# Two blocks of w_in ahead of the first batch's x in the load queue, and another transfer model in the planner

## The chip, the cores and the metric

The program runs on one core of one Trainium2 chip. The metric is the device time of one execution in microseconds (us). The core has a matrix engine (PE, with its weight loads, PEld), a vector engine (DVE), an activation engine (ACT), a general engine (POOL), and a queue engine (SP) that here issues every transfer. Each engine takes its instructions strictly in the order in which they were written; an instruction that waits holds up all behind it on that engine.

## What is computed

Three stages in a row, in float32 inputs and outputs; the three weight matrices of the second and third stage come as float64.

```python
def _attn_ref(x, state):                       # x 8x8x512x64, state 8x8x32x64
    scores = scale * np.matmul(x, state.transpose(0, 1, 3, 2))
    a = softmax(scores); xread = np.matmul(a, state)
    scores2 = scale * np.matmul(state, x.transpose(0, 1, 3, 2))
    a2 = softmax(scores2); sread = np.matmul(a2, x)
    return np.concatenate([xread, sread], axis=2)

def _moe_ref(x, w_in, w_out, g_ln):            # 4352 tokens, 512 -> 1024 -> 512
    h = x @ w_in
    solu = h * softmax(h)
    ln = (solu - mean) / sqrt(var + 1e-06) * g_ln
    return ln @ w_out

def _moe2_ref(x, w_in, w_out):                 # 512 -> 2048 -> 512
    r = np.maximum(x @ w_in, 0.0)
    return (r * r) @ w_out
```

## The kernel before

**Phase 1** goes through eight batches of 512 tokens and then the 256 state tokens. Per batch: `scores` (PE products of `bdf`, the states, and `xT`, the transposed x; ACT copies them to `s_sb`), `max_t` (a DVE maximum, tile `m`), `emit_sT` (PE transposes; DVE maximum `mx` and subtraction into `a_sb`; ACT exponential in place; DVE sum, reciprocal; POOL scales), `emit_aT` (PE transposes back; ACT copies to `aT`), `emit_sw` (states times w_in, so that attention and the first dense layer become one product), `emit_l1` (PE products of `sw` and `aT` into `hps`; DVE maximum `hm`, ACT copy `u`), `solu_rest` (two ACT passes over 1024 columns with a DVE product between them, then POOL and DVE), `emit_lnT` (transposes, then ACT and DVE write the two halves of `lt`), and `emit_l2` (PE products of `lt` and `wo` into `y`). Beside that run `exp_t`, `emit_e`, `sread` and `emit_xs` for the state rows: ACT `eT`, PE `ep`, ACT copy back into `s_sb`, PE `srd`, ACT `sr`, PE `xsp`. Phase 1's results go to DRAM (`y_d`).

**Phase 2** runs over 9 groups of 512 (the last: 256) rows and 16 blocks `m` of 128 columns: `emit_l3` (PE products `h` of `wa[m]` and `yt`, line 907), `relu2` (ACT `r`, DVE `r*r`, ACT cast to the high part of `g`, DVE subtraction for its low part), and two steps later `emit_l4` (PE products `o` of `g` and `wb[m]`, line 922). Of each three products one needs the low part of `g`. The next group's rows come back from DRAM in two halves (`yraw`), which ACT casts and DVE or POOL subtracts (`yt`).

**The weights** are float64, so each block of 128x512 is loaded as 512 KB and decoded (`decode`): one ACT pass (line 293), two DVE passes (lines 296 and 299), for most weights an ACT cast into the high part and a subtraction into the low part, on POOL or DVE (line 249). The eight w_in blocks go to eight buffers of the pool `up`, so all eight can be in flight; they are the tiles `wi`, four for the first 512 columns (c = 0) and four for the rest. w_out's eight blocks (`wo`) follow; six can be in flight. Half of the third stage's weights are decoded in phase 1 and parked in DRAM; the other half (m = 8 to 15) are decoded in phase 2's first steps, with three `raw` buffers, which the halves of `yraw` share: a transfer is issued when the DVE pass that read its buffer has ended.

**What sets the order.** PE's order is written out by hand. The order on ACT, DVE, POOL and SP comes from a planner (`Flow`) while the program is built: it keeps a clock of its own, with a cost for each piece of work, and gives each engine the piece that is ready and due first; a second pass uses the due times that the first found. A transfer of `kb` KB is taken to occupy the resource "D" for kb/360 us, after earlier transfers, and to be ready 2.0 us later (`run`). The names of the steps below are the ones of the code. At the program's start SP issues the states and x of batch 0 (`load_x(0)`), then the eight w_in blocks, then `xn` (`load_xn(0)`), then w_out.

Of the kernel before, what the change touches and what calls it, by code (L numbers as in the profile page):

```python
# [23 lines left out]
class Flow:  # L24
# [16 lines left out]
    def __init__(self, plan=None):  # L41

        self.plan, self.made = plan, []
        self.now = 0.0
        self.end = 0.0
        self.warm = self.WARM_UP
        self.free = {"V": 0.0, "A": 0.0, "P": 0.0, "D": 0.0}
        self.tasks = []

    def run(self, eng, cost, ready, emit):  # L50
# [98 lines left out]
def attn_solu_relu2_kernel(  # L149
# [14 lines left out]
    nc = tc.nc  # L164
# [6 lines left out]
    B, P, T, _ = x_n.shape  # L171
    S = x_t.shape[3]
    HP = x_t.shape[2]
    H, D = 2 * HP, P // 2
# [13 lines left out]
    fl = Flow(plan)  # L188
# [33 lines left out]
    room = {"raw": 3, "dec": 3, "e": 2, "raw2": 3, "dec2": 2}  # L222

    def dma(out, in_, kb):
        return fl.run("D", kb / 360.0, 0.0, lambda e: nc.sync.dma_start(out=out, in_=in_))

    def take(name):
        def ok():
# [36 lines left out]
    def decode(dst_h, dst_l, src, pool=None, w=None, spare=False):  # L265

        raw, dec = ("raw2", "dec2") if spare else ("raw", "dec")
        if pool is None:
            yield take(raw)
            t = (ap_ if spare else raw_p).tile(
                [P, 512, 2], I32, tag=raw, name="raw", bufs=3
            )
        else:
            t = pool.tile([P, 512, 2], I32, tag="u", name="raw_u")
        tf = t.rearrange("p n c -> p (n c)")
        src = src.bitcast(I32)  # L280
        if len(src.shape) == 3:
            tf = tf.rearrange("p (k f) -> p k f", k=src.shape[1])
        f = dma(tf, src, 512)
        own = w is None
        if own:
            yield take(dec)
            w = (ap_ if spare else dec_p).tile(
                [P, 512], F32, tag=dec, name="dec", bufs=2 if spare else 3
            )
        w_i = w.bitcast(I32)  # L290
        hi, lo = t[:, :, 1], t[:, :, 0]
        h = hi.bitcast(F32)
        f = yield {"A": 0.66}, f, lambda e: nc.scalar.activation(
            out=w, in_=h, func=AF.Prelu, scale=2.0 ** -112, alpha=-(2.0 ** 32)
        )
        f = yield {"V": 0.46}, f, lambda e: nc.vector.tensor_scalar(  # L296
            out=w_i, in0=w_i, scalar1=3, scalar2=None, op0=ALU.logical_shift_left
        )
        f = yield {"V": 0.69}, f - fl.HOP, lambda e: nc.vector.scalar_tensor_tensor(  # L299
            out=w_i, in0=lo, scalar=29, in1=w_i, op0=ALU.logical_shift_right, op1=ALU.bitwise_or  # L300
        )
        if pool is None:
            give(raw)
        if not own:
            return f
        f = yield from split_w(dst_h, dst_l, w, f)
        give(dec)
        return f
# [14 lines left out]
    def load_x(b):  # L323
        bdf[b] = ap_.tile([P, G, 192], F32, tag="bdf", name="bdf", bufs=2)
        done["st", b] = dma(bdf[b], bd[b], 192)
        xT[b] = ap_.tile([P, HP, S], F32, tag="xT", name="xT")
        done["xT", b] = dma(xT[b], x_t[b], 1024)
# [439 lines left out]

    make_identity(nc, ident)
    nc.vector.memset(mhalf, -0.5)
    load_x(0)  # L770
    for c in range(C1):
        for k in range(KD):
            cs = slice(c * 512, (c + 1) * 512)
            done["wi", k, c] = fl.spawn(decode(
                None, None, w_in[k * P:(k + 1) * P, cs], pool=up, w=wi[k][:, cs],
            ), 5.0)
# [227 lines left out]
```

## Time and profile before

| what | value |
|---|---|
| time, median of 3 runs (range) | 1179.89 us (1179.64 to 1179.99) |
| profiled execution, its own time | 1181.55 us |
| its span, first to last instruction | 1179.5 us |
| PE busy | 1145.5 us (97%) |
| DVE, ACT, POOL busy | 534.7, 490.9, 177.8 us |
| PE's share of the chain that ended last | 90% |
| mean granted clock of PE | 0.991 |

PE is nearly always busy, so only its remaining gaps and its stretches at the lower granted clock can be won or widened. "Granted clock" (PEclk) is the share of full speed: 1.00 is 2.4 GHz, 0.50 is 1.2 GHz. PE's idle time lies in three places: the program's first 60 us, about one microsecond per batch in phase 1, and one gap at 470 us in phase 2.

### The profile page before, as it was taken

To read this page: it belongs to the slowest core of one execution; us is meant where nothing else is said; L and a number is where in the kernel's file an instruction comes from. 1 tells how busy PE (TensorE), PEld (TensorE's weight loads), DVE (VectorE), ACT (ScalarE), POOL (GpSimd) and SP (SyncE) were. 2 spreads that over 40 slices of the span, in tenths; PEclk is the share of its full clock that TensorE was granted. 3 is DMA by queue.
4 is the path that set the end of the run, shared out by engine and by line. 5 is a ranking of instruction groups with operands and counts; after the bars stand their busy time and mean duration, and the time that the engine had idled before them with its cause. 6 is when DMAs were issued, how large, how long until landed. Compare 5 with 4: busy or idle time off the path is not lost.

```text
span 1179.5 us, 14989 instructions
## 1 busy us (share of the span) xinstructions
PE 1145.5 (97%) x5992; PEld 910.7 (77%) x5992; DVE 534.7 (45%) x866; ACT 490.9 (42%) x875; POOL 177.8 (15%) x217
## 2 busy tenths in 40 slices
PE   4799999999999999999999999999999999999998
PEld 1377777777777687788888888888888888888887
DVE  6776876867764449423233232233232232232232
ACT  5866776767665456322222232232232232222222
POOL 1441433333243204100000000000000000010000
PEclk8999999999999999999999999999999999999999
DMA  9323253362331746011010020020020020010010
GB/s 358 126 79 111 94 186 108 114 214 77 111 121 63 298 144 214 18 33 40 1 51 21 1 72 1 1 72 1 1 72 1 1 72 1 1 54 1 1 37 18
DMA packets 32309, 88.00 MB, mean 75 GB/s; under 512 B 3824, under 2 KB 13040, under 8 KB 30192
## 3 DMA queue, kind: packets, MB, share of 16 engines
q1 hardware_dynamic: 32240, 87.05, 21.5%
q8 instruction: 47, 0.77, 0.3%
q14 instruction: 22, 0.18, 0.1%
HBM read 60.82 MB, written 26.21 MB: 74 GB/s over the span
## 4 chain that ended last, share of the span: by engine, by line
PE 90%; DVE 4%; ACT 3%; DMA 2%; issue 1%; SPq 0%; POOL 0%; ACTq 0%; DVEq 0%; POOLq 0%
PE o L922 31%; PE h L907 31%; PE y L675 14%; PE hps L614 8%; PE lnTp L640 2%; PE hps L360 1%; DMA raw<-w_in 1%; DMA raw_u<-w_in 1%; PE sTp L399 1%; DVE dec L299 1%; PE srd L471 1%; DVE hm L550 1%; ACT e L585 1%; DVE dec L296 1%; PE aTp L455 0%
## 5 line engine op out<-in xcount | busy, mean ns | idle before, releaser
L922 PE MATMUL o<-wb,g 128*128 128x512 f32 x1632 | 395.4, 391 | 2.9 <-ACT g L243 2.6
L907 PE MATMUL h<-yt,wa 128*128 128x512 f32 (+1 forms) x1728 | 394.2, 377 | 0.0
L907 PEld LDWEIGHTS h<-yt,wa 128*128 128x128 f32 x1728 | 313.3, 188 | 61.1
L922 PEld LDWEIGHTS o<-wb,g 128*128 128x128 f32 x1632 | 306.3, 189 | 66.8 <-ACT g L243 3.0
L891 DVE TENSOR_TENSOR r<-r 128x512 f32<-128x512 f32 (+1 forms) x144 | 109.0, 757 | 395.8 <-ACT r L884 395.7
L884 ACT ACTIVATE r<-h 128x512 f32<-128x512 f32 (+1 forms) x144 | 82.5, 573 | 405.5 <-PE h L907 405.3
L675 PE MATMUL y<-lt,wo 128*128 128x512 f32 (+1 forms) x864 | 218.8, 395 | 2.0 <-ACT lt L646 1.6
L675 PEld LDWEIGHTS y<-lt,wo 128*128 128x128 f32 x864 | 149.1, 190 | 38.5 <-issue 8.4
L249 DVE TENSOR_TENSOR g<-r,g 128x512 fp32r<-128x512 f32 (+1 forms) x144 | 95.6, 664 | 81.8 <-ACT g L243 76.0
L243 ACT CAST g<-r 128x512 fp32r<-128x512 f32 (+1 forms) x144 | 86.0, 597 | 101.8 <-DVE r L891 100.8
L249 POOL TENSOR_TENSOR yt<-yraw,yt 128x1024 fp32r<-128x1024 f32 (+1 forms) x8 | 18.2, 2277 | 558.2 <-ACT yt L243 558.2
L614 PE MATMUL hps<-sw,aT 128*128 128x512 f32 x368 | 97.9, 415 | 0.0
L614 PEld LDWEIGHTS hps<-sw,aT 128*128 128x128 f32 x368 | 69.0, 189 | 23.6 <-issue 6.8
L649 DVE SCALAR_TENSOR_TENSOR lt<-lnTp,g_sb,lt 128x512 fp32r<-128x512 f32 (+1 forms) x72 | 51.1, 710 | 38.4 <-ACT lt L646 38.0
L550 DVE TENSOR_REDUCE hm<-hps 128x1 f32<-128x512 f32 x68 | 45.8, 688 | 44.1 <-PE hps L614 34.8
L243 ACT COPY u<-hps 128x512 f32<-128x512 f32 x68 | 39.6, 582 | 55.1 <-DVE hm L550 54.9
L646 ACT ACTIVATE lt<-lnTp,g_sb 128x512 fp32r<-128x512 f32 (+1 forms) x72 | 47.9, 667 | 12.6 <-PE lnTp L640 12.6
L579 DVE SCALAR_TENSOR_TENSOR u<-u,e 128x1024 f32<-128x1024 f32 x34 | 42.5, 1251 | 9.9 <-ACT e L574 9.9
L585 ACT ACTIVATE e<-u,nmu 128x1024 f32<-128x1024 f32 x34 | 39.2, 1152 | 15.8 <-DVE nmu L582 14.9
L640 PE MATMUL lnTp<-ident,u 128*128 128x128 f32 x272 | 41.8, 274 | 1.6 <-DVE a_sb L249 1.2
L640 PEld LDWEIGHTS lnTp<-ident,u 128*128 128x128 f32 x272 | 32.7, 140 | 11.1 <-issue 2.4
L574 ACT ACTIVATE e<-u,nmx 128x1024 f32<-128x1024 f32 x34 | 39.1, 1150 | 3.0 <-DVE nmx L567 2.9
(83 smaller groups left out, 714.7 us busy)
## 6 DMA issues: line engine op xcount, KB each, us to landing
raw<-w_out SPq DMA_DIRECT2D x24, 512.0 KB, 5.2
out<-osb SPq DMA_DIRECT2D x34, 256.0 KB, 2.2
xT<-x_t SPq DMA_DIRECT2D x8, 1024.0 KB, 4.9
xn<-x_n SPq DMA_DIRECT2D x8, 1024.0 KB, 6.6
y_d<-ys SPq DMA_DIRECT2D x16, 512.0 KB, 2.9
raw<-w_in SPq DMA_DIRECT2D x16, 512.0 KB, 4.3
w_d<-w2s SPq DMA_DIRECT2D x16, 512.0 KB, 3.0
yraw<-y_d SPq DMA_DIRECT2D x16, 512.0 KB, 5.5
```

The costliest lines, as they stand in the source:

```text
L243: nc.scalar.copy(out=out, in_=in_)
L249: return lambda e: eng_of[e].tensor_tensor(out=out, in0=in0, in1=in1, op=ALU.subtract)
L550: one({"V": 0.68}, lambda e, c=c, ps=ps: nc.vector.tensor_reduce(out=m2[:, c:c + 1], in_=ps, axis=AX.X, op=ALU.max)),
L585: f = yield {"A": 1.16}, f, lambda e: nc.scalar.activation(out=e_, in_=u, func=AF.Square, bias=nmu, accum_out=vs)
L614: nc.tensor.matmul(out=ps, lhsT=lhsT(i, k), rhs=rhs(j, k)[:, cs], start=(k == 0 and n == 0), stop=(k == n_k - 1 and n == len(passes) - 1),)
L640: nc.tensor.transpose(ps[:, t, :], u_t[key, t][:, k * P:(k + 1) * P], ident)
L649: f = yield {"V": 0.1 + nt * 0.155}, f, lambda e: nc.vector.scalar_tensor_tensor(out=o[:, 1], in0=pf, scalar=gk, in1=o[:, 0].bitcast(F32), ...
L675: nc.tensor.matmul(out=ps, lhsT=wo[k][:, w, c * P:(c + 1) * P], rhs=o[:, a], start=(k == 0 and i == 0), stop=(k == K1 - 1 and i == 2),)
L884: first = one({"A": 0.06 + n / 1000}, lambda e: nc.scalar.activation(out=r, in_=hps, func=AF.Relu))
L891: f = yield {"V": 0.15 + n / 960}, first["done"], lambda e: nc.vector.tensor_tensor(out=r, in0=r, in1=r, op=ALU.mult)
L907: nc.tensor.matmul(out=hps, lhsT=wa[m][:, w, k, :], rhs=yt[j][:, a, k, :], start=(k == 0 and i == 0), stop=(k == KD - 1 and i == 2),)
L922: nc.tensor.matmul(out=ops[j][t], lhsT=g[:, a, t * P:(t + 1) * P], rhs=wb[m][:, w, :], start=(m == 0 and i == 0), stop=(m == K2 - 1 and i ...
```

## The change

Batch 0's states and x are issued after the first two w_in blocks. The planner's transfers become faster (400 instead of 360 KB per us), and the first cannot start before 2.2 us. Since all orders but PE's come from the planner, both numbers reorder work all over the program. PE's order is the same as before, row for row.

```diff
-        self.free = {"V": 0.0, "A": 0.0, "P": 0.0, "D": 0.0}
+
+        self.free = {"V": 0.0, "A": 0.0, "P": 0.0, "D": 2.2}
...
-        return fl.run("D", kb / 360.0, 0.0, lambda e: nc.sync.dma_start(out=out, in_=in_))
+        return fl.run("D", kb / 400.0, 0.0, lambda e: nc.sync.dma_start(out=out, in_=in_))
...
-    load_x(0)
     for c in range(C1):
         for k in range(KD):
+            if (c, k) == (0, 2):
+                load_x(0)
```

Behind the new lines each line number is one or two higher than before.

**Place 1: the start.** DVE before, from the first w_in block on (`wi_122` to `wi_125` are the four w_in tiles, `m` the maximum of the scores, the last row the subtraction of the first half):

```order
L296 TENSOR_SCALAR wi_122<-wi_122 128x512
L299 SCALAR_TENSOR_TENSOR wi_122<-raw_u,wi_122 128x512
L371 TENSOR_REDUCE m_202<-s_sb 128x1
L296 TENSOR_SCALAR wi_123<-wi_123 128x512
L299 SCALAR_TENSOR_TENSOR wi_123<-raw_u,wi_123 128x512
L296 TENSOR_SCALAR wi_124<-wi_124 128x512
L299 SCALAR_TENSOR_TENSOR wi_124<-raw_u,wi_124 128x512
L371 TENSOR_REDUCE m_214<-s_sb 128x1
```

and now:

```order
L297 TENSOR_SCALAR wi_122<-wi_122 128x512
L300 SCALAR_TENSOR_TENSOR wi_122<-raw_u,wi_122 128x512
L297 TENSOR_SCALAR wi_123<-wi_123 128x512
L300 SCALAR_TENSOR_TENSOR wi_123<-raw_u,wi_123 128x512
L297 TENSOR_SCALAR wi_124<-wi_124 128x512
L300 SCALAR_TENSOR_TENSOR wi_124<-raw_u,wi_124 128x512
L372 TENSOR_REDUCE m_209<-s_sb 128x1
L297 TENSOR_SCALAR wi_125<-wi_125 128x512
```

The first maximum moved from behind the first block to behind the third. ACT a little later, before (`dec<-raw` is the first pass over a w_out block, `a_sb` the exponential of the second half):

```order
L243 COPY sw<-hps 128x512
L293 ACTIVATE wi_125<-raw_u 128x512
L243 COPY sw<-hps 128x512
L418 ACTIVATE a_sb<-a_sb 128x512
L243 COPY aT<-aTp 128x512
L293 ACTIVATE dec<-raw 128x512 x3
```

and now:

```order
L294 ACTIVATE wi_125<-raw_u 128x512
L244 COPY sw<-hps 128x512
L294 ACTIVATE dec<-raw 128x512
L419 ACTIVATE a_sb<-a_sb 128x512
L244 COPY aT<-aTp 128x512
L294 ACTIVATE dec<-raw 128x512 x3
```

The first pass over w_out's first block moved ahead of the exponential.

**Place 2: the end of batch 0's first layer.** ACT before, from the last but one pass over 1024 columns ahead of the copy of `ep` (wo_129 to wo_131 are w_out's fourth to sixth block):

```order
L574 ACTIVATE e,es<-u,nmx 128x1024
L243 COPY u<-hps 128x512
L574 ACTIVATE e,es<-u,nmx 128x1024
L243 COPY s_sb<-ep 128x512
L243 COPY u<-hps 128x512
L585 ACTIVATE e,vs<-u,nmu 128x1024
L574 ACTIVATE e,es<-u,nmx 128x1024
L489 ACTIVATE sr<-srd,l_186 128x64 x2
L349 ACTIVATE s_sb<-sps 128x512
```

and now:

```order
L586 ACTIVATE e,vs<-u,nmu 128x1024
L244 COPY u<-hps 128x512
L586 ACTIVATE e,vs<-u,nmu 128x1024
L244 COPY u<-hps 128x512
L244 COPY s_sb<-ep 128x512
L575 ACTIVATE e,es<-u,nmx 128x1024 x2
L244 CAST wo_131<-dec 128x512
L350 ACTIVATE s_sb<-sps 128x512
L490 ACTIVATE sr<-srd,l_186 128x64 x2
```

The last two exponentials moved behind the copy of `ep`, and the casts of w_out's fifth and sixth block came into this stretch from a later one, where one of them stood just ahead of the first `lt`.

**Place 3: phase 2, where the last w2 blocks and the next group's `yraw` come in.** ACT before (`r_4730` and `g_4731` are those of block m = 6 of the first group):

```order
L243 CAST wa15_4434<-dec_4687 128x512
L243 CAST yt_4481<-yraw_4704 128x1024
L884 ACTIVATE r_4730<-h2_4701 128x512
L243 CAST wb13_4431<-dec_4707 128x512
L293 ACTIVATE dec_4726<-raw_4720 128x512
L243 CAST g_4731<-r_4730 128x512
L243 CAST yt_4481<-yraw_4735 128x1024
```

and now (`r_4737` and `g_4738` are the same block):

```order
L244 CAST wa15_4434<-dec_4679 128x512
L244 CAST yt_4486<-yraw_4691 128x1024
L244 CAST wb13_4431<-dec_4695 128x512
L886 ACTIVATE r_4737<-h2_4709 128x512
L294 ACTIVATE dec_4715<-raw_4712 128x512
L244 CAST yt_4486<-yraw_4728 128x1024
L244 CAST g_4738<-r_4737 128x512
```

The cast of the second half of `yraw` moved ahead of the cast of `g`, and on DVE its subtraction moved ahead of the low part of `g` in the same way. In the steps before, the first pass of a w2 block stands one block earlier against `r` and `g`, and one subtraction (wa11's) went from DVE to POOL. In phase 1's batches 2 to 5, likewise, a w2 block's first pass and cast stand ahead of a `u` copy and an `lt`.

## Rows read from the trace of the kernel before

**Rows 1.** Windows: stretch, its length, busy us (count) per engine, PEclk, DMA.
```profile
20.00:30.00 10.00, 5.90 (x25) 2.11 (x24) 9.61 (x16) 6.85 (x13) 3.62 (x3) 0.50 1.05 388
...
47.00:59.00 12.00, 7.42 (x65) 3.77 (x57) 9.62 (x20) 11.20 (x26) 7.09 (x13) 0.86 0.53 192
...
61.00:64.00 3.00, 3.00 (x10) 2.41 (x10) 2.97 (x5) 1.10 (x3) 2.13 (x2) 0.50 0.02 5
...
434.00:470.00 36.00, 36.00 (x160) 29.52 (x158) 33.61 (x42) 24.00 (x41) 15.35 (x11) 1.00 0.69 218
...
474.00:477.00 3.00, 3.00 (x8) 2.33 (x8) 3.00 (x3) 1.60 (x4) 1.80 (x1) 0.50 0.01 4
...
480.00:1150.00 670.00, 670.00 (x3002) 556.62 (x3001) 197.83 (x277) 173.15 (x284) 18.17 (x8) 1.00 0.08 23
```

**Rows 2.** Waits of PE from 70 us to the end: total us, times, longest.
```profile
PE sTp L399 <- ACT s_sb L243: 4.4, 6, 0.7
```

**Rows 3.** Timeline of ACT at the start: start, us, what, [idle before <- releaser].
```profile
9.88 0.66 ACT L293 ACTIVATE wi<-raw_u 128x512 f32<-128x512 f32 x1 [0.85 <-DMA raw_u<-w_in]
...
11.34 0.68 ACT L293 ACTIVATE wi<-raw_u 128x512 f32<-128x512 f32 x1 [0.32 <-DMA raw_u<-w_in]
...
20.66 0.63 ACT L418 ACTIVATE a_sb<-a_sb 128x512 f32<-128x512 f32 x1 [1.73 <-DVE a_sb L249]
...
21.67 0.67 ACT L293 ACTIVATE dec<-raw 128x512 f32<-128x512 f32 x1
22.81 0.68 ACT L293 ACTIVATE dec<-raw 128x512 f32<-128x512 f32 x1 [0.47 <-DMA raw<-w_out]
```

**Rows 4.** Timeline of DVE at the start.
```profile
8.51 0.43 DVE L296 TENSOR_SCALAR wi<-wi 128x512 int32<-128x512 int32 x1 [7.67 <-ACT wi L293]
...
18.13 1.90 DVE L296 TENSOR_SCALAR wi<-wi 128x512 int32<-128x512 int32 x3
```

**Rows 5.** Timeline of PE at the start.
```profile
24.42 1.11 PE L455 MATMUL aTp<-ident,a_sb 128*128 128x128 f32 x4 [4.10 <-POOL a_sb L428]
```

**Rows 6.** Timeline of PE and ACT from 42.9 to 60 us.
```profile
42.95 0.60 PE L442 MATMUL ep<-ident,eT 128*128 128x128 f32 x4
...
43.73 1.16 ACT L574 ACTIVATE e<-u,nmx 128x1024 f32<-128x1024 f32 x1
...
44.87 0.58 ACT L243 COPY s_sb<-ep 128x512 f32<-128x512 f32 x1
...
45.50 0.65 PE L471 MATMUL srd<-xn,s_sb 128*32 128x64 f32 x32 [1.37 <-ACT s_sb L243]
...
58.23 0.63 ACT L243 CAST wo<-dec 128x512 fp32r<-128x512 f32 x1
...
59.50 0.73 PE L675 MATMUL y<-lt,wo 128*128 128x512 f32 x2 [1.57 <-ACT lt L646]
```

**Rows 7.** Timeline of all engines from 464 to 474 us.
```profile
464.21 0.34 SPq L225 DMA_DIRECT2D yraw<-y_d  x1
...
467.92 0.33 SPq L225 DMA_DIRECT2D yraw<-y_d  x1
468.00 1.05 ACT L243 CAST yt<-yraw 128x1024 fp32r<-128x1024 f32 x1 [0.55 <-DMA yraw<-y_d]
...
472.02 0.62 ACT L243 CAST g<-r 128x512 fp32r<-128x512 f32 x1 [0.97 <-DVE r L891]
...
472.69 0.73 PE L922 MATMUL o<-wb,g 128*128 128x512 f32 x2 [2.58 <-ACT g L243]
472.88 1.05 ACT L243 CAST yt<-yraw 128x1024 fp32r<-128x1024 f32 x1 [0.24 <-DMA yraw<-y_d]
472.96 0.68 DVE L249 TENSOR_TENSOR g<-r,g 128x512 fp32r<-128x512 f32 x1
473.70 4.16 PE L922 MATMUL o<-wb,g 128*128 128x512 f32 x10 [0.28 <-DVE g L249]
...
473.96 1.23 DVE L249 TENSOR_TENSOR yt<-yraw,yt 128x1024 fp32r<-128x1024 f32 x1 [0.31 <-ACT yt L243]
```

## The prediction

> **What bounds the kernel now.** I read the windows first [rows 1]: from 434 to 470 us and from 480 to 1150 us PE is busy without a gap, so nothing that the change moves there counts unless it is late enough to open one. Over the whole of 70 us to the end, the list of PE's waits has, beside the gap at 470, little more than one entry: 0.7 us in six batches, for a copy that waits for PE itself [rows 2]. So a change of order on the other engines can move the time in three places: the start, the stretch to 60 us where ACT is the full engine (11.20 of 12 us in the window from 47 us [rows 1]), and the gap of 2.58 us at 470 us in phase 2 [rows 7]. In the first and the third the granted clock matters as well. It was 0.50 from 20 to 30 us, from 61 to 64 us and from 474 to 477 us [rows 1], each time behind a stretch in which PE had waited, and it was 1.00 in the full stretches. In a 0.50 stretch PE does half the work, so being late there costs half, and a wait that falls into one costs half of itself.
>
> The sum below is made against the profiled execution, 1181.55 us with a span of 1179.5. The median of the runs is 1179.89, so a difference found there is carried over to the median as it is. A measurement of this kernel can tell about 0.2%, 2.4 us, from no change.
>
> **Part A, the start.** The third w_in block has the same bytes ahead of it as before (states, x, two blocks), so it still arrives at about 11.3 us [rows 3], and so do all transfers behind it. What changes hands are the places in front: the first two blocks now come before 9.9 us, and x comes where the second block came, at about 9.9 us [rows 3]. The gain: the DVE passes over two blocks fall into time in which DVE sat idle for 7.67 us [rows 4]. The price: x's scores come later, and their first maximum, a pass of about 0.7 us, now stands behind the third block, in the stretch in which DVE had no room. Part of that is covered, since three passes of 0.42 us took 1.90 us there, 0.6 us of it waiting [rows 4]. So the subtraction of the second half comes 0 to 0.7 us later. It is not what decides. ACT's exponential of that half, which started at 20.66, now stands behind the first pass over w_out's first block. That pass ran at 21.67, and its block had only just come: the second came at 22.81, after a wait; at 1.46 us from block to block (11.34 less 9.88) the first came at 21.35 or later, and at 21.67 at the latest, so about 21.5 [rows 3]. The exponential then starts at 21.5 + 0.6 = 22.1 instead of 21.1 at the least: about 1.0 to 1.4 us later than 20.66, of which I take 1.0, because the passes queued on DVE cover the rest. The chain behind it (DVE sum, POOL, PE's transpose at 24.42 [rows 5]) moves with it: 25.4. PE runs at 0.50 until 30 us [rows 1], so 1.0 us late is 0.5 us of work at full clock. **A: +0.5**, between 0 (transfers that start quicker) and +1.0 (no halving).
>
> **Part B, 30 to 62 us.** The copy of `ep` stood behind an exponential that ran from 43.73 to 44.87, though PE had ended `ep` at 43.55; PE waited 1.37 us for that copy and went on at 45.50 [rows 6]. Now two exponentials stand behind the copy instead, so with A's 0.5 the copy can start at 44.05 to 44.5: 0.4 to 0.8 earlier, of which A's delay has been taken. Against this, the casts of w_out's fifth and sixth block, 0.63 each [rows 6], come into a stretch in which ACT is full, ahead of the copies of the scores for which PE waits next. The fifth's left a place at 58.23, right before the first `lt`, for which PE waited until 59.50 [rows 6], but a first pass of 0.67 takes that place. So PE's first `y` product comes between 0.6 earlier (the copy's gain) and 1.3 later (both casts). Around 61 to 64 us the clock is 0.50 [rows 1], so half of it counts. And A's half microsecond is partly lost in this part anyway, since ACT, not PE, sets its pace. **B: -0.2**, between -0.8 and +0.7.
>
> **Part C, phase 2 at 470 us.** Before, ACT cast `g` of block 6 at 472.02, PE went on at 472.69 with the products that need only the high part, waited again, and went on at 473.70 when the low part (472.96 + 0.68) was there [rows 7]. ACT's cast of the second half of `yraw` came after it, at 472.88, as soon as that transfer had landed. Now this cast stands ahead. The transfer is issued when a DVE pass has freed its buffer, at 467.92, and cannot be cast before 472.88 if DVE gets there no sooner. DVE is busy 33.61 of the 36 us before [rows 1], with the same passes in another order: one subtraction (0.7) fewer, and one more on POOL, during which DVE's passes get longer. I take no change of pace, 0.7 either way. Then: cast of `yraw` 472.88 to 473.93, cast of `g` to 474.55, subtraction of `yraw` on DVE (1.23) from 473.96 to 475.15, low part of `g` to 475.75. PE goes on with the low part at 475.75 instead of 473.70: 2.05 later. Any wait that the later `g` of block 5 opens falls inside this one, since PE only gets to the same gate later. The clock gives some back: from 474 to 477 it was 0.50 with PE busy throughout [rows 1], and now PE stands still for about half of that, if the low stretch stays where it was. A second low stretch behind the longer wait would take that and more. I give back 0.7. **C: +1.3**, between +0.3 (landing and DVE earlier, all of the clock's gift) and +2.8 (2.05 and a low stretch moved onto full work).
>
> A transfer of 512 KB took 3.8 us from issue to its cast at the one place and 5.0 at the other [rows 7], more than the planner's 3.28. The Trainium skill speaks for the planner here: DMA: Bandwidth & Descriptors, section Anatomy of one DMA, has about 2.0 us of fixed cost plus the bytes at 436 GB/s, which would be an estimated 3.2 us. By that figure the second half would have landed at 471.1 us and the new place of its cast would cost next to nothing; the trace does not agree, and the measured 5.0 decides.
>
> **Part D, the rest.** In four batches a w2 block's first pass and cast (0.67 + 0.62) stand ahead of an `lt`. PE waited for no `lt` after 70 us: the only entry of weight is another copy [rows 2], so the cover is the work that PE has queued; without it each would cost up to 0.7. I take 0, between -0.3 and +1. In phase 2's later groups the casts of `yraw` move ahead of `r`; PE has no gap there [rows 1], and `g` is due two steps later, so 0.
>
> **The sum.** +0.5 - 0.2 + 1.3 + 0 = +1.6 us: 1183.15 us for an execution like the profiled one (span 1181.1), and 1179.89 + 1.6 = **1181.5 us** for the median, which is 0.14% and inside what counts as the same. With the parts' bounds half used on either side, this case reaches from 1179.9 to 1183.5.
>
> **The rivals.**
>
> *The wait at 470 us grows in full (slower).* One mechanism: the `yraw` cast holds up `g`, and the clock falls after the wait rather than during it. C is then 2.8, A and B together +0.8: 1179.89 + 3.6 = 1183.5. For it: DVE was nearly full before 470 us, and blocks are decoded one step earlier against `r` and `g`, so that `g` of block 5 comes late too. Against it: in the trace the low stretch began at 474, in the wait's wake, and a longer wait overlaps it. It decides from the point where PE's restart passes about 476 us.
>
> *The start wins (faster).* Mechanism: DVE's early passes and a quicker start of the transfers pull the second half's exponential ahead rather than behind, and the copy of `ep` 0.8 earlier carries through to the first `y`, so that the wait before 59.50 (1.57) goes and with it the low stretch from 61 to 64 us, which holds 3 us at half speed and so costs 1.5. That is -0.8 - 0.8 - 1.5 = -3.1, plus at the least 0.3 for C: 1177.1. For it: 7.67 us of idle DVE at the start is the largest gap that the change can fill. Against it: the first pass over w_out stands ahead of the exponential and is bound to a transfer that does not come earlier.
>
> *Nothing that counts.* Transfers land as the planner has them, 3.8 us as the first half did: the second half lands at 467.92 + 3.8 = 471.7, its cast ends at 472.8, PE's low part comes at 474.6, 0.9 later than before, half of it at 0.50, and A and B cancel: 1180.3. This is also the skill's figure made into a mechanism, with its time from the rows.
>
> **How the numbers follow.** Forecast 0.36, slower rival 0.34, faster rival 0.18, nothing that counts 0.12. The edges are 1177.5 and 1182.25 us. Of the forecast's 0.36 I count 0.07 as beyond the upper edge and 0.02 beyond the lower, and of the slower rival's 0.34 I count 0.05 inside: slower 0.36, faster 0.17 (a little of it falls short of the edge), same 0.47. The range for 8 in 10 reaches into both rivals: from 1177.4 to 1185.0, the upper end being the slower rival with A and D at their bounds (+1.5).
>
> **What would show it.** Right in A: the second `aTp` of the start at about 25.4, behind an exponential that follows a pass over w_out. Right in B: PE's second `srd` between 44.6 and 45.2, first `y` within 1 us of 59.5. Right in C: in phase 2, ACT's `yraw` cast directly ahead of `g`, PE waiting for `g` about 2 us longer at 470 to 476, and the low part behind a subtraction of `yraw`. Wrong in C, and the forecast with it: PE's wait there no longer than 2.9 us in all, or two low stretches of the clock instead of one. Wrong in A and B: PE's first `y` before 58.5 or after 61, or the low stretch at 61 us gone.

## The result

| kernel | median us (runs) | ratio to before, 95% interval | PE's first `h` of phase 2, us | from there to the end of the span, us |
|---|---|---|---|---|
| before | 1179.94 (4) | 1 | 429.12 | 750.4 |
| after | 1193.55 (4) | 1.0107 (1.0095 to 1.0119) | 435.66 | 756.5 |

The changed kernel is 13.6 us slower by the medians. Its profiled execution took 1193.97 us, with a span of 1192.2 us, which is 12.7 us more than the span of before; the places of the loss below are read from these two profiles. The forecast was 1181.5 us, with a range up to 1185.0: the time lies far outside it.

PE runs the same products in the same order in both, so the start of one and the same product is a ruler. One profile stands for each kernel: seven profiles with the same start as after put the first `y` at 60.07 to 60.74 us, so differences of less than about 0.7 us say little. PE's first product of phase 2, in before and then in after:

```profile
429.12 8.34 PE L907 MATMUL h<-yt,wa 128*128 128x512 f32 x36
```

```profile
435.66 8.34 PE L909 MATMUL h<-yt,wa 128*128 128x512 f32 x36
```

Phase 1 thus lost 6.5 us and phase 2 another 6.2. At the first `y` (59.50 before [rows 6], 60.12 after) only 0.6 was lost, so the batches carry 5.9. After's windows (columns as in [rows 1]) over the batches and at the beginning of phase 2:

```profile
64.00:440.00 376.00, 365.73 (x2402) 276.56 (x2401) 233.45 (x429) 236.28 (x442) 114.46 (x163) 1.00 0.37 129
440.00:500.00 60.00, 52.97 (x217) 41.62 (x216) 45.80 (x55) 32.01 (x54) 21.13 (x15) 0.94 0.47 151
```

PE's waits in after from 70 us to the end (total, times, longest), where before had the entry of [rows 2], 0.9 us for `sw`, and the gap of [rows 7]:

```profile
PE sTp L400 <- ACT s_sb L244: 4.8, 6, 1.2
PE o L924 <- DVE g L250: 3.8, 3, 1.4
PE o L924 <- ACT g L244: 3.2, 2, 3.0
PE hps L615 <- ACT s_sb L350: 2.8, 3, 1.3
...
PE hps L615 <- ACT u L244: 0.6, 1, 0.6
```

The chain that ended last, PE's at 90% in before, now reads:

```profile
PE 80%; DVE 7%; DMA 7%; ACT 5%; issue 2%; SPq 0%; ACTq 0%; DVEq 0%
```

New are the waits of `hps` for `s_sb` and `u`; those for the low part of `g` grew from 0.3 to 3.8 us. All of these are written by ACT or DVE behind something else. What that is, ACT's own waits from 70 to 440 us show: before, then after.

```profile
ACT dec L293 <- DMA raw<-w_in: 12.0, 6, 3.7
ACT dec L293 <- DMA raw<-w_out: 7.4, 3, 3.1
```

```profile
ACT dec L294 <- DMA raw<-w_in: 14.4, 5, 3.8
ACT dec L294 <- DMA raw<-w_out: 12.7, 5, 3.8
```

ACT stands idle for weight blocks that have not landed, 19.4 us before (1.3 of it, at 440 us, for a block of phase 2, the rest for parked blocks) and 27.1 us after, and behind some of these passes PE's work queues up. The largest single case, after, all engines from 154 to 172 us:

```profile
155.08 0.33 SPq L226 DMA_DIRECT2D xn<-x_n  x1
...
155.50 0.41 SPq L226 DMA_DIRECT2D w_d<-w2s  x1
...
156.01 0.38 SPq L226 DMA_DIRECT2D raw<-w_out  x1
...
165.08 0.66 ACT L294 ACTIVATE dec<-raw 128x512 f32<-128x512 f32 x1 [3.83 <-DMA raw<-w_out]
165.64 0.57 ACT L244 COPY u<-hps 128x512 f32<-128x512 f32 x1
...
166.26 1.66 PE L615 MATMUL hps<-sw,aT 128*128 128x512 f32 x6 [0.55 <-ACT u L244]
...
166.95 0.62 ACT L244 CAST w2s<-dec 128x512 fp32r<-128x512 f32 x1 [0.15 <-DVE dec L300]
167.48 1.15 ACT L575 ACTIVATE e<-u,nmx 128x1024 f32<-128x1024 f32 x1
...
168.62 0.57 ACT L350 ACTIVATE s_sb<-hps 128x512 f32<-128x512 f32 x1
...
169.25 1.68 PE L615 MATMUL hps<-sw,aT 128*128 128x512 f32 x6 [1.33 <-ACT s_sb L350]
```

The block is issued behind a 1 MB load and a 512 KB store and lands 9.0 us later. ACT comes to its pass at 161.25, waits 3.83, and only then copies the second `u`, which PE waits for; the cast and the exponential behind it make `s_sb` late, and PE waits again. Ahead of this place PE was 0.86 us later than in before (its `y` products start at 164.05 against 163.19), behind it 3.32 us (its next transposes start at 170.76 against 167.44), so 2.5 of the batches' 5.9 us are lost here. In before ACT has done `u`, `lt` and the exponential by the time it comes to the same pass, the transfer has landed, 7.9 us after its issue, and PE's products are in one piece:

```profile
161.16 0.59 ACT L243 COPY u<-hps 128x512 f32<-128x512 f32 x1 [0.78 <-DVE hm L550]
161.65 0.69 ACT L646 ACTIVATE lt<-lnTp,g_sb 128x512 fp32r<-128x512 f32 x1
...
162.23 1.15 ACT L574 ACTIVATE e<-u,nmx 128x1024 f32<-128x1024 f32 x1
...
163.36 0.66 ACT L293 ACTIVATE dec<-raw 128x512 f32<-128x512 f32 x1
...
164.69 2.91 PE L614 MATMUL hps<-sw,aT 128*128 128x512 f32 x12
```

In phase 2, after, all engines around the `yraw` cast that the prediction spoke of:

```profile
467.72 2.57 PE L924 MATMUL o<-wb,g 128*128 128x512 f32 x10 [1.25 <-DVE g L250]
...
475.29 2.57 PE L924 MATMUL o<-wb,g 128*128 128x512 f32 x10 [1.37 <-DVE g L250]
...
477.34 0.33 SPq L226 DMA_DIRECT2D yraw<-y_d  x1
...
478.46 1.65 DVE L893 TENSOR_TENSOR r<-r 128x512 f32<-128x512 f32 x1
...
482.00 1.04 ACT L244 CAST yt<-yraw 128x1024 fp32r<-128x1024 f32 x1 [3.02 <-DMA yraw<-y_d]
482.95 0.61 ACT L244 CAST g<-r 128x512 fp32r<-128x512 f32 x1
483.08 1.23 DVE L250 TENSOR_TENSOR yt<-yraw,yt 128x1024 fp32r<-128x1024 f32 x1 [1.91 <-ACT yt L244]
...
483.62 1.22 PE L924 MATMUL o<-wb,g 128*128 128x512 f32 x2 [3.04 <-ACT g L244]
...
484.16 1.27 POOL L250 TENSOR_TENSOR wb<-dec,wb 128x512 fp32r<-128x512 f32 x1 [4.61 <-ACT wb L244]
484.22 1.76 DVE L250 TENSOR_TENSOR g<-r,g 128x512 fp32r<-128x512 f32 x1
...
486.04 4.53 PE L924 MATMUL o<-wb,g 128*128 128x512 f32 x10 [1.20 <-DVE g L250]
```

`r` was squared by 480.11, so `g` could have been cast then; it stood behind a transfer that landed at 482.00. A window over 484 to 491 us shows what followed, PE at about half of its clock (0.55) for 7 us, where before had 3 us of it [rows 1]:

```profile
484.00:491.00 7.00, 5.80 (x15) 4.08 (x15) 5.60 (x8) 3.49 (x7) 2.55 (x2) 0.55 0.00 0
```

### The profile page after: what moved, and what is told of

The parts are those of the page before. It is cut to its first block, busy times and chain, and to the rows that moved or that the text cites. A ratio compares the mean times of both kernels' runs of the same rounds, so it can differ in the third digit from the quotient of the medians.

```text
span 1192.2 us, 14996 instructions
## 1 busy us (share of the span) xinstructions
PE 1147.1 (96%) x5992; PEld 910.0 (76%) x5992; DVE 533.7 (45%) x865; ACT 489.4 (41%) x875; POOL 173.6 (15%) x218
## 4 chain that ended last, share of the span: by engine, by line
PE 80%; DVE 7%; DMA 7%; ACT 5%; issue 2%; SPq 0%; ACTq 0%; DVEq 0%
PE o L924 30%; PE h L909 29%; PE y L676 11%; PE hps L615 6%; DMA raw<-w_out 3%; DMA raw<-w_in 3%; PE lnTp L641 2%; DVE dec L300 1%; DVE dec L297 1%; DVE u L580 1%; DVE hm L551 1%; ACT u L244 1%; ACT dec L294 1%; PE hps L361 1%; DMA xT<-x_t 1%
## 5 line engine op out<-in xcount | busy, mean ns | idle before, releaser
L893 DVE TENSOR_TENSOR r<-r 128x512 f32<-128x512 f32 (+1 forms) x144 | 98.9, 687 | 373.1 <-ACT r L886 372.9
L250 DVE TENSOR_TENSOR g<-r,g 128x512 fp32r<-128x512 f32 (+1 forms) x144 | 105.9, 735 | 85.6 <-ACT g L244 79.8
L294 ACT ACTIVATE dec<-raw 128x512 f32<-128x512 f32 x40 | 26.9, 673 | 39.4 <-DMA raw<-w_in 19.4
```

The lines of the kernel that those rows point to most:

```text
L250: return lambda e: eng_of[e].tensor_tensor(out=out, in0=in0, in1=in1, op=ALU.subtract)
L893: f = yield {"V": 0.15 + n / 960}, first["done"], lambda e: nc.vector.tensor_tensor(out=r, in0=r, in1=r, op=ALU.mult)
```

## The experiments

The theory (**late passes**): the planner believes transfers ready earlier than they land, so it puts passes and casts of incoming data ahead of work for PE on engines that cannot step over them; the faster rate does it in more places. The main rival (**start**): the new load order at the start sets off the rest. The first two kernels divide the change into its parts. The 2.2 us are part of e1 and are not run by themselves. All results stand in one table behind the last experiment; the kernel before was run beside each group, with medians from 1180.6 to 1181.3 us, and the ratios are to those.

**e1_load_order**, the changed kernel with

```diff
-        return fl.run("D", kb / 400.0, 0.0, ...
+        return fl.run("D", kb / 360.0, 0.0, ...
```

> The changed kernel with the planner's transfers back at 360 KB per us; the load order and the 2.2 us stay. Its orders are those of the kernel before but for the first 45 rows of ACT and 63 of DVE. Theory (late passes): the loss comes from passes over weight blocks that the faster model puts ahead of work for PE, so this one stands at 1180 us, within 1 us of the kernel before (at 64 us the changed kernel's PE was 0.1 us late). Rival (start): the new start sets off the rest, and 1184 us or more is measured.

Measured: 1180.21 us, no different from before (the rival asked for 1184 or more). **e2_rate**, the kernel before with 400 in the same line:

> The kernel before with 400 instead of 360 KB per us in the planner and nothing else; the 2.2 us does nothing without the new load order and is left out. Its orders are those of the changed kernel but for the first 20 rows of ACT and DVE. Theory (late passes): 1193 us, within 1 us of the changed kernel, since the batches and phase 2 carry the whole loss. Rival (start): under 1188 us, the rest being the start's.

Measured: 1193.42 us, as slow as the changed kernel (1.0104 times before, against 1.0107). The rate carries the loss, and the start falls as its cause.

**e3_yraw_behind_g** exchanges the two casts in phase 2:

```diff
-            f = dma(t, src[:, cs, :], n)
+            f = dma(t, src[:, cs, :], n) + (1.0 if (j, c2) == (1, 1) else 0.0)
```

> The changed kernel with one exchange: in phase 2's first group the cast of the second half of yraw stands behind the cast of g of block 6 on ACT, and its subtraction behind g's low part on DVE (the planner is told that this one transfer is ready 1.0 us later); all else is row for row the same. In the changed kernel PE waited 3.04 us for that cast of g and 1.20 for its low part. Theory (late passes): g is cast when DVE has squared r, at about 480.2 instead of 482.95, PE goes on at about 480.9 and with the low part at 482 instead of 486.0, so 3 to 4 us are won: 1189.5 to 1190.5 us. Rival (the wait only moves): the rows behind, yt or the next block, make PE wait instead, and under 1 us is won.

Measured: 1189.22 us, 4.3 us under the changed kernel. In its profile, the fastest of its four runs (1187.70 us), phase 2 is 5.1 us shorter (751.4). PE's rows there:

```profile
479.43 0.74 PE L924 MATMUL o<-wb,g 128*128 128x512 f32 x2 [0.59 <-ACT g L244]
480.44 2.56 PE L924 MATMUL o<-wb,g 128*128 128x512 f32 x10 [0.28 <-DVE g L250]
```

The waits of 3.04 and 1.20 are now 0.59 and 0.28, and the ten products take 2.56 instead of 4.53: the low clock is gone as well (granted 1.00 from 440 to 500 us, 0.94 in after and 0.97 in before). So this exchange wins back 5.1 of phase 2's 6.2 us. But it does so in part by removing the gap and the low stretch that before had at this place too, and the loss at the two blocks ahead of it is still there: the table under Part C shows both.

**e4_one_block_later** moves one block's pass, the one of 165 us; **e5_blocks_later** moves those of all sixteen by 2.0 us:

```diff
-            yield from decode(th, tl, src)
+            yield from decode(th, tl, src, late=1.0 if i == 3 else 0.0)   # e5: late=2.0
...
-        f = dma(tf, src, 512)
+        f = dma(tf, src, 512) + late
```

> The changed kernel with one of the parked blocks, the fourth, counted ready 1.0 us later by the planner: its first pass, for which ACT stood idle 3.83 us at 165 us, then stands behind the copy of u, the lt and the exponential; 10 rows of ACT, 26 of DVE, 10 of POOL and 2 of SP differ, between 150 and 172 us, and nothing else. In the changed kernel PE fell 2.4 us behind there (waits of 0.55 for u and 1.33 for s_sb). Theory (late passes): both waits go, and PE at 169 us is 0.8 us behind the kernel before instead of 3.2: 1191 us, with the rest of the loss as it was. Rival (transfers themselves, or work in sum): PE loses the same there, 1193 us.

> The changed kernel with all sixteen parked blocks counted ready 2.0 us later by the planner; the start and everything from phase 2 on stand as in the changed kernel. With the fourth block alone 1.0 us later the whole was 1190.76 us. Theory (late passes): PE's loss between 64 and 440 us, 6.5 us to the first wait of phase 2, falls under 1.5 us: 1187 to 1189 us, with phase 2's loss left. Rival (the other orders of the batches, the stores ahead of the next states among them, carry it): over 1190 us.

Measured: 1190.76 and 1186.11 us, the second a little below its range. With one block later, ACT's pass runs without a wait and PE's products are in one piece:

```profile
164.25 0.66 ACT L294 ACTIVATE dec<-raw 128x512 f32<-128x512 f32 x1
```

```profile
165.58 2.91 PE L615 MATMUL hps<-sw,aT 128*128 128x512 f32 x12
```

The single block was worth 2.7 us at phase 2's start (432.93 against 435.66). All blocks together bring PE there at 426.63, 9.0 us earlier than in the changed kernel and 2.5 earlier than in the kernel before (by the medians 7.4 us are won, since phase 2 takes 0.8 longer in this profile); PE's waits from 64 to 450 us are down to one entry:

```profile
PE sTp L400 <- ACT s_sb L244: 4.4, 6, 0.7
```

**e6_not_waited_for** asks whether it is the wait or the work put ahead. Every instruction keeps its place:

```diff
+        if other is not None:      # wo[0], long resident
+            hi, lo = o2[:, :, 1], o2[:, :, 0]
...
-            yield from decode(th, tl, src)
+            yield from decode(th, tl, src, other=wo[0])
```

> The changed kernel with every instruction in its place and every transfer issued, but the first and the last pass over each of the sixteen parked blocks read the resident tile of w_out's first block instead of the loaded buffer, so that ACT and DVE wait for none of these transfers (the parked weights, and so the third stage's results, are not the right ones). Theory (late passes, by the wait): the batches' loss goes as in e5_blocks_later, since the passes and casts themselves cost PE next to nothing where they stand: 1186.5 to 1189 us. Rival (late passes, by the work): the 0.67 and 0.62 us of work ahead of u and lt are the price, not the idle time: 1191.5 us or more.

Measured: 1184.45 us, below the theory's range, and PE at phase 2's start at 426.70, within 0.1 us of e5. The order stayed, the waits went, and the whole loss of the batches went with them: it was the wait, not the work (and 2.5 us more came back, which before had been losing in the same way). The pass of 165 us now runs where it stands:

```profile
161.41 0.67 ACT L297 ACTIVATE dec<-wo 128x512 f32<-128x512 f32 x1
```

**e9_yraw_not_waited_for** asks the same of phase 2:

```diff
+            if (j, c2) == (1, 1):
+                t = yt[0][:, 0, cs].bitcast(F32)
             f = yield {"A": 0.09 + n / 480}, f, copy(yt[j][:, 0, cs], t)
```

> The changed kernel with every instruction in its place and every transfer issued, but the cast and the subtraction of the second half of the second group's yraw read the first group's yt instead of the loaded buffer, so that ACT does not stand idle for this transfer (3.02 us in the changed kernel); the second group's results are not the right ones. Theory (late passes, by the wait): the cast runs as soon as ACT comes to it, at about 479, and g behind it at about 480.2 instead of 482.95: 3 to 5 us won, 1188.5 to 1190.5 us, as in e3_yraw_behind_g. Rival (by the work): the cast of 1.05 and the subtraction of 1.23 ahead of g are the price: under 1.5 us won, 1192 us or more.

Measured: 1190.53 us; phase 2 is 3.1 us shorter than in the changed kernel (753.5), where e3 had made it 5.1 shorter. PE and DVE:

```profile
478.73 0.73 PE L926 MATMUL o<-wb,g 128*128 128x512 f32 x2 [0.24 <-ACT g L244]
...
480.14 1.75 DVE L250 TENSOR_TENSOR g<-r,g 128x512 fp32r<-128x512 f32 x1
...
481.95 3.44 PE L926 MATMUL o<-wb,g 128*128 128x512 f32 x10 [2.49 <-DVE g L250]
```

PE's wait for the cast of `g` is gone (0.24), but its low part, behind `yraw`'s subtraction of 1.22 and itself 1.75 long, now costs 2.49. So of what e3 wins in phase 2, about 3 us are the wait, and 2 us the work ahead of `g`, in which POOL's lengthening of the low part has its share. The time lies at the upper edge of the theory's range, and a part of the rival holds.

**e7_both_later**, e5's and e3's edits together:

> The two exchanges together: the sixteen parked blocks 2.0 us and the second half of yraw 1.0 us later in the planner, all else as in the changed kernel. Theory (late passes): the gains add. e3_yraw_behind_g won 4 to 6 us, e5_blocks_later should win 5, so 1182 to 1184 us, 1 to 3 us above the kernel before, by the waits of 1.2 and 1.4 us for g's low part that phase 2 still holds. Rival: the gains overlap (PE that is earlier at 440 us waits longer in phase 2): 1185 us or more.

Measured: 1180.43 us, the time of the kernel before, with the rate of 400 and the new load order left in. The gains add, to a little more than was expected (1182 to 1184).

**e8_y_at_eight** was an attempt at the gap of [rows 7] itself, on e1:

```diff
-            if m == 2 and j + 1 < len(groups):
+            if m == 8 and j + 1 < len(groups):
```

> e1_load_order with the next group's yraw asked for at block 8 of a group instead of block 2, so that in the first group its casts and subtractions stand behind the last weight blocks. In e1_load_order PE waited 2.6 us for the cast of g at that place. Theory (late passes): the two casts of 1.05 and two subtractions of 1.23 us were what made g late, so the wait falls under 1 us and the low stretch of the clock behind it goes: 1177 to 1178.5 us. Rival (the weight blocks themselves make g late: casts of the last blocks now stand ahead of it): the wait stays over 2 us, 1180 us.

Measured: 1181.51 us, so the rival holds. Without `yraw` the weight blocks take its place ahead of `r` and `g` (two rows of DVE, one of PE):

```profile
468.32 1.65 DVE L300 SCALAR_TENSOR_TENSOR dec<-raw,dec 128x512 int32<-128x512 int32 x1
...
469.89 0.68 DVE L893 TENSOR_TENSOR r<-r 128x512 f32<-128x512 f32 x1
...
471.39 0.73 PE L924 MATMUL o<-wb,g 128*128 128x512 f32 x2 [2.37 <-ACT g L244]
```

**e10_old_rate_later** is e1 with e5's edit; **e11_all_ready_later** and **e12_before_ready_later** give the planner one other number, e11 in the changed kernel and e12 in the kernel before:

```diff
-        return start + cost + (2.0 if eng == "D" else self.HOP)
+        return start + cost + (5.0 if eng == "D" else self.HOP)
```

> e1_load_order (360 KB per us) with the sixteen parked blocks counted ready 2.0 us later; phase 2 as in the kernel before. Theory (late passes): the kernel before has the same fault in a smaller measure, ACT idle 18.1 us for blocks between 70 and 430 us; in e7_both_later PE was 1.9 us ahead of the kernel before at 335 us by the same change, so about 2 us under e1_load_order: 1178.2 us. Rival (that gain is taken back by phase 2's wait at 470 us): 1180 us.

> The changed kernel, 400 KB per us, with every transfer of the planner counted ready 5.0 instead of 2.0 us after its last byte. Theory (late passes): no pass is put ahead of PE's work for a transfer that has not landed, in phase 1 and 2 alike: 1178 to 1182 us. Rival (it's the exact order, not lateness in general, that counts; passes too late hold up buffers and the weights' transfers behind them): over 1184 us.

> The kernel before, its load order and its 360 KB per us, with every transfer counted ready 5.0 instead of 2.0 us after its last byte, and nothing else. e11_all_ready_later, with the same number in the changed kernel, came to 1173.73 us. Theory (late passes): what is in the way is the planner's too early readiness, in both kernels, so this one gains as much: 1172.5 to 1176 us. Rival (the load order or the rate of 400 has its share in that gain): 1177 us or more.

Measured: 1177.84, 1173.73 and 1168.79 us, the last two below what was expected, and all a little faster than the kernel before (by 0.3 to 1.1%). In e12 PE has one entry left in its list of waits from 70 us on, and no gap from 440 to 500 us:

```profile
PE sTp L399 <- ACT s_sb L243: 1.5, 2, 0.7
```

```profile
64.00:440.00 376.00, 374.00 (x2459) 287.57 (x2458) 251.96 (x448) 247.93 (x457) 114.65 (x161) 1.00 0.39 136
440.00:500.00 60.00, 60.00 (x266) 49.71 (x265) 40.29 (x48) 27.75 (x48) 16.92 (x12) 1.00 0.33 106
```

| kernel | median us (runs) | ratio to before, 95% interval | first `h` of phase 2 | to the end |
|---|---|---|---|---|
| e1_load_order | 1180.21 (10) | 0.9992 (0.9983 to 1.0002) | 428.00 | 750.1 |
| e2_rate | 1193.42 (4) | 1.0104 (1.0087 to 1.0121) | 435.03 | 756.2 |
| e3_yraw_behind_g | 1189.22 (4) | 1.0069 (1.0052 to 1.0085) | 434.53 | 751.4 |
| e4_one_block_later | 1190.76 (4) | 1.0081 (1.0066 to 1.0096) | 432.93 | 755.5 |
| e5_blocks_later | 1186.11 (4) | 1.0043 (1.0029 to 1.0058) | 426.63 | 757.3 |
| e6_not_waited_for | 1184.45 (5) | 1.0034 (1.0021 to 1.0047) | 426.70 | 756.0 |
| e7_both_later | 1180.43 (10) | 0.9996 (0.9986 to 1.0005) | 426.55 | 751.5 |
| e8_y_at_eight | 1181.51 (10) | 1.0005 (0.9996 to 1.0015) | 427.99 | 752.3 |
| e9_yraw_not_waited_for | 1190.53 (4) | 1.0088 (1.0073 to 1.0104) | 434.22 | 753.5 |
| e10_old_rate_later | 1177.84 (7) | 0.9973 (0.9962 to 0.9983) | 424.15 | 749.8 |
| e11_all_ready_later | 1173.73 (4) | 0.9939 (0.9926 to 0.9953) | 426.03 | 745.5 |
| e12_before_ready_later | 1168.79 (4) | 0.9894 (0.9878 to 0.9911) | 420.69 | 745.3 |

What stays open: why e12 is 4.9 us faster than e11. They differ in load order with its 2.2 us, and in rate. 2.7 us of it are there at the first `y` (58.33 against 61.06), the rest comes in the batches, where PE waits five times for the `s_sb` copy in e11 (3.7 us) and twice in e12 (1.5). The rate is the likelier part at the first `y`: every profile at 360 has it at 58.06 to 59.50 us and every profile at 400 at 59.89 to 61.06, under either load order. But no run separates the two at the new readiness.

## Why the prediction was wrong, step by step

**The sum** put 0 into the batches and 1.3 into phase 2; they cost 5.9 and 6.2. Its list of what would show it wrong had no sign for the batches at all. For phase 2 it named a wait of no more than 2.9 us, or two low stretches of the clock instead of one; there were 7.0 us of waits and one low stretch of twice the length. Two slips in the working are too small to matter: in part C 473.96 + 1.23 + 0.68 is 475.87 and not 475.75, and half of the parts' lower bounds leads to 1180.3 and not 1179.9.

**Part A** (+0.5) came near in its sum, but by luck. After's rows at the start, and at the two points that part B named:

```profile
24.75 1.11 PE L456 MATMUL aTp<-ident,a_sb 128*128 128x128 f32 x4 [3.69 <-POOL a_sb L429]
...
46.29 0.86 PE L472 MATMUL srd<-xn,s_sb 128*32 128x64 f32 x32 [2.25 <-ACT s_sb L244]
...
60.12 2.44 PE L676 MATMUL y<-lt,wo 128*128 128x512 f32 x4 [1.12 <-ACT lt L647]
```

The second `aTp` came at 24.75, 0.33 us later than before and not at 25.4: the first w_out block was there at 20.84, half a microsecond before the earliest time that I had worked out from the spacing of two blocks [rows 3]. And the 0.6 us by which the first `y` is late do not go with the load order: in e1, with the same load order at 360, it starts at 58.06, and in e2, with the old load order at 400, at 59.89. **Part B** (-0.2): the first `y` came within the bound, at 60.12, but the second `srd` at 46.29 and not before 45.2. The copy of `ep` did lose its two exponentials, but stood now behind another pass over 1024 columns (43.64 to 44.80) and a copy of `u` that waited 0.28 for DVE's maximum, which I had not followed, though both stand in the list of place 2. Both parts are small: 0.6 us at the first `y`.

**Part D** is the step that failed worst. It read PE's waits of the kernel before [rows 2], found none for an `lt`, and called the passes moved ahead covered, at 0.67 and 0.62 us each, so 0 in sum; the batches lost 5.9. The price of such a pass is not its duration but its start: on an engine that runs in order, everything behind it inherits the wait for its transfer. e6 shows this apart from all else: with every row in its place, and no pass waiting for these transfers, PE is 9.0 us earlier at phase 2's start, more than the 5.9 that the batches had lost. The row that would have told it stood in the trace of before, and I did not ask for it: ACT's waits, not PE's. ACT already stood idle there, 18.1 us for blocks of this kind, and that cost something too: counting the blocks later under the old rate (e10) brings PE to phase 2 3.9 us earlier than in e1. I had looked at the issue of a w2 block nowhere, and priced the transfer only in phase 2.

A change in the planner's rate looks too small to matter. For the block of 165 us the planner counts, from the first of the three transfers, (1024 + 512 + 512)/400 + 2.0 = 7.1 us, or 6.2 after the block's own issue 0.93 later; at 360 it is 6.8 (estimates, since the planner's clock is not the chip's). The block took 9.0 us in after and 7.9 in before. That rate alone moves such passes is shown by e2. That it was these 0.6 us which put this pass ahead of `u`, `lt` and the exponential is argued, not shown; counting the block 1.0 us later moved it back and won 2.7 us (e4). Why the same transfer took 1.1 us longer in after is not settled.

**Part C** had the mechanism at the gate, where PE waits for `g`, and missed most of what phase 2 lost. The cast did stand directly ahead of `g`, and the low part behind `yraw`'s subtraction. Where the 6.2 us went, the starts of the same products show. "Later" is counted from each kernel's own first `h` of phase 2, against before:

| PE's product | before, us | after, us | after, later by | e3, us | e3, later by |
|---|---|---|---|---|---|
| first `h` of phase 2 | 429.12 | 435.66 | 0 | 434.53 | 0 |
| second to last `h` before the gate | 461.78 | 470.13 | 1.81 | 468.55 | 1.36 |
| last `h` before the gate | 467.23 | 477.70 | 3.93 | 475.95 | 3.31 |
| `o` at the gate, high part | 472.69 | 483.62 | 4.39 | 479.43 | 1.33 |
| `h` behind the gate | 477.70 | 490.41 | 6.17 | 482.83 | -0.28 |

So 3.9 of the 6.2 us are lost at the two blocks of `o` ahead of the gate, where PE waited 1.25 and 1.37 us for the low part and 0.18 for `g`. The prediction let every such wait fall inside the one at the gate, and that is the step of part C that failed: the gate's own wait did not shrink for it (3.04 against 2.58), because the transfer came later too. The second half of `yraw` was issued 41.68 us into phase 2 instead of 38.80, where I had taken no change of pace, 0.7 either way; its own 4.66 us (477.34 to 482.00) were close to the 5.0 assumed. Behind the gate another 1.8 us went. From `g`'s cast to its low part I had 1.2 us, measured were 2.4, since the subtraction of 0.68 took 1.76 beside one on POOL, so that PE waited 1.20 for it and not 0.28. And the clock, from which I took 0.7 back, cost instead: about 7 us at half speed instead of 3, of which PE was busy in 5.8. What makes the low part late at the two blocks ahead is read from the rows alone: at 465.41, for one, a weight block's second DVE pass, 1.66 long beside POOL, stands ahead of it. No run moves these passes by themselves; in e11 and e12, with all of them later, no wait for `g` is left.

**The rivals.** "The wait at 470 us grows in full" came nearest, with 2.8 us for phase 2 against 6.2, and it too had nothing for the batches. "The start wins" was not seen: e1 is within 0.2% of before. "Nothing that counts" rested on transfers as fast as the planner's, and fell with that.

**What the first part called the bound** was wrong as well. It took PE's gaps in the batches for about a microsecond each that PE itself sets (e12 leaves two of the six), and the long full stretches as proof that little could be won. e12 wins 8.4 us by phase 2's start and 5.1 after it. PE's list of waits added up to 5.3 us between 70 and 440 us in before, and e12's PE, which keeps 1.5 us of such waits, gains 7.3 between the first `y` and phase 2: the list is not a ledger, the start of the same product in two traces is.

The Trainium skill, DMA: Bandwidth & Descriptors, section Anatomy of one DMA, has a fixed 2.0 us and the bytes at 436 GB/s for one transfer issued on GpSimd's path, which the planner's model resembles; the transfers here are issued by SP, which the prediction passed over. By it a 512 KB transfer would take an estimated 3.2 us, and the three of 155 us together an estimated 6.8 from the first issue. The trace agrees with neither: the half of `yraw` took 4.66 us, beside other blocks, and the three were there 10.0 us after the first issue (155.08 to 165.08). It is not short everywhere: the sixteen 512 KB stores of `y` between 60 and 440 us landed after a median of 2.9 us in either kernel, the loads of weight blocks after medians of 4.4 to 6.5. A planner that uses such a figure for loads that queue with others is early, as it was at both places.

## What to carry over

Where an in-order engine takes work that waits for a transfer, price the step with everything queued behind it, and read that engine's own waits for transfers before trusting that the matrix engine shows none. In a planner like this one, the readiness of a transfer should lean to the late side: here one microsecond more gave 2.7 us back at one place (e4), and three more everywhere won 12.5 (e12). How much later still pays, no run shows. When two kernels run the same products in the same order, set the ledger by the start of one product, not by lists of waits.

## What the hardware showed beside that

A DVE pass over 128x512 with two inputs that takes 0.68 to 0.69 us by itself took 1.65 (478.46) and 1.76 (484.22) in the rows above while POOL ran a subtraction: the low part of `g` ran beside one on POOL from 484.16 to 485.43. The Trainium skill, Trainium Architecture — The Big Picture, section What this means for kernel authors, says that DVE and GpSimd share a pair of ports under an exclusive lock; the trace agrees in that this pass, begun at 484.22, is 1.07 longer, most of the 1.21 that POOL still had to run. It means that moving a subtraction to POOL is not free for DVE, which the prediction had named without a price.
